# Linear attention and a feed-forward layer in one kernel: d_ff in five stretches with scales of their own, and the first pair's groups taken through them in parts

## The chip, the cores and the metric

The kernel runs on one core of a Trainium2 chip, as one program. The metric is the device time of one execution in microseconds, so smaller is better. Three runs of the kernel before gave 717.43, 718.17 and 720.17; the median is 718.17.

## What is computed

The reference, cut to what matters (8 batches, 8 heads, 576 tokens, heads of 64, 32 memory slots; d_model 512, d_ff 2048):

```python
a = softmax of phi over the 576 tokens             # phi: (8, 8, 576, 32)
k_m = np.einsum('bhsm,bhsd->bhmd', a, k)
v_m = np.einsum('bhsm,bhsd->bhmd', a, v)
attn = softmax of (q @ k_m^T / 8) over the 32 slots
x = attn @ v_m, heads side by side                 # 4608 tokens x 512
h = x @ w_in                                       # 4608 x 2048
g = h * np.cos(h)
out = (g @ w_out).astype(np.float32)               # 4608 x 512
```

Everything comes in as float32 but for the two weight matrices, which the kernel reads as 64-bit floats (pairs of 32-bit words).

## The kernel before, in words

**Work.** The 4608 tokens are taken in 12 groups of 384. Two batches (a pair) make three groups: all of the first group is from the first batch, the second is shared half and half, the third is from the second batch. For each group, d_ff goes by in 16 chunks of 128, so the whole has 192 steps. A step (`gemm1`, `act`, `act_end`, `gemm2`, lines 480 to 543) is:

- TensorE makes hp, 128 d_ff rows by 384 tokens, from the attention weights aT and from vw. vw is v_m folded into w_in beforehand (256 by 2048 for a batch), so that x is never made.
- ScalarE makes u, h in turns plus a quarter (L503). VectorE casts u to whole numbers (L508) and subtracts these (L509). ScalarE takes the sine, which is cos(h) (L513). VectorE multiplies by h (L517). ScalarE casts the product to float16 (L519), and VectorE makes the remainder, a second float16 part (L520).
- Four steps later (`LAG`), TensorE multiplies both parts with w_out into three accumulators of 128 tokens by 512 (L538). After chunk 15, ScalarE copies the three out of PSUM (L554) and they are stored.

**Parts.** From the second group on, a float32 product is made of three float16 products (first by first, first by second, second by first part): 6 matmuls of 384 columns for hp, 9 of 512 for the accumulators. The powers of two that bring the parts into range come from the largest sums of squares of all of w_in and all of w_out (`weight_scale`, L162), so they are known only when all weights are there. The first group doesn't wait for that: it works in float32, 2 matmuls for hp (L485) and 3 for the accumulators (L533), each of which the profile lists as two. Its fold (`fold_first`, L448) gives float32 too.

**Weights.** There are 8 loads of w_in (256 columns each) and 8 of w_out (256 rows each), 1 MB each. `to_float32` (L124) makes float32 of one load with three ScalarE operations (L135, L139, L142, the last with the sum of squares) and two of VectorE (L133, L140). In the first group every step converts one load (`convert_next`, L627). In the second group each step splits a block of w_out (L178, L179) and a quarter of a slice of w_in (L189, L190), whose parts then go by DMA to both halves of the partitions (L200, L201).

**Order.** The kernel is written engine by engine in program order, step by step, with the next batches' attention (`memory`, `attend`) and folds spread over the steps by a table (`jobs`, `folds`). A scheduling layer then fixes the order of each engine's queue; each engine works its own queue in that order, so an instruction that waits holds up all behind it. hp has three PSUM banks, the accumulators three, the small tiles (scores, folds) two. `make_identity` builds the unit matrix ident on GpSimd; the first use of ident is the product `top` (L223), which spreads the maximum of phi.

Of the kernel before, what the change touches and what calls it, by code (L numbers as in the profile page):

```python
# [37 lines left out]
BLK_FIRST = [(0, 256), (256, GT - 256), (GT, S - GT)]  # L38
TWO_PI_BELOW = 6.283185
# [6 lines left out]
def attention_then_ffn(ctx: ExitStack, tc: tile.TileContext, phi, phiT, kv, qT, w_in, w_out, out):  # L46
# [13 lines left out]
    make_identity(nc, ident)  # L60
    # in X, heads of even number hold [k | v] and those of odd number [v | k]
# [5 lines left out]
    w_in_sb = const.tile([P, NP, DF], F32, name="w_in_sb")  # L67
    # w_out: block f + 1 holds rows f * 128 on as float32, later block f their two float16 parts
    wo = const.tile([P, NF + 1, DM], F32, name="wo")

    def wo_parts(f):
        return wo[:, f].bitcast(F16).rearrange("p (w e) -> p w e", w=2)

    vl = const.tile([P, NP, 2, M], F16, name="vl")
# [32 lines left out]
    def load_w_in(j):  # L107
        if j in (2, 3):
            # the space of w_out's last blocks, which come later
            t = wo[:, 13:17] if j == 2 else wo[:, 9:13]  # L110
            t = t.bitcast(I32).rearrange("p c (f t) -> p c f t", t=2)
        else:
            t = ld.tile([P, NP, WS, 2], I32, tag=next_raw(), name=f"raw_in_{j}")
        nc.sync.dma_start(out=t, in_=w_in[:, 2 * WS * j:2 * WS * (j + 1)].rearrange("(c p) (f t) -> p c f t", p=P, t=2))
        loads["in", j] = t

    def load_w_out(j):
        t = ld.tile([P, 2, DM, 2], I32, tag=next_raw(), name=f"raw_out_{j}")
# [3 lines left out]
    sq = const.tile([P, 2, NW], F32, name="sq")  # L122
# [21 lines left out]
    def convert_w_in(j):  # L144
        to_float32(w_in_sb[:, :, j * WS:(j + 1) * WS], loads.pop(("in", j)), sq[:, 0, j:j + 1], j == 1)

    def convert_w_out(j):
        to_float32(wo[:, 2 * j + 1:2 * j + 3], loads.pop(("out", j)), sq[:, 1, j:j + 1])

    # e, a power of two, with every magnitude below 2 e; and 2^14 / e  # L150
# [11 lines left out]
    def weight_scale(kind, name):  # L162
        # halving the exponent of the largest sum of squares
        m = const.tile([P, 1], F32, name=f"m_{name}")
        nc.vector.tensor_reduce(out=m, in_=sq[:, kind], op=ALU.max, axis=AX.X)
        nc.gpsimd.partition_all_reduce(m, m, channels=P, reduce_op=RED.max)
        nc.vector.tensor_scalar(out=m, in0=m, scalar1=2.0, scalar2=2.0 ** -100, op0=ALU.mult, op1=ALU.max)
        nc.vector.tensor_scalar(out=m.bitcast(I32), in0=m.bitcast(I32), scalar1=1, scalar2=None,
                                op0=ALU.logical_shift_right)
        nc.vector.tensor_scalar(out=m, in0=m, scalar1=2.0 ** 63, scalar2=None, op0=ALU.mult)  # L170
        e = const.tile([P, 1], F32, name=f"e_{name}")
        power_of_two(e, m)
        st["e", name] = e
        st["s", name] = to_range(f"s_{name}", const, f"s_{name}", e)

    def w_out_split(f):
        parts, s = wo_parts(f), st["s", "out"]
# [7 lines left out]
    def w_in_split(q, c):  # L185
        if c == 0:
            st["parts"] = ld.tile([P, 2, NP, FS], F16, tag=f"raw{1 + q % 2}", name=f"w_in_parts_{q}")
        parts, s, src = st["parts"], st["s", "in"], w_in_sb[:, c, q * FS:(q + 1) * FS]
        nc.scalar.activation(parts[:, 0, c], src, AF.Copy, scale=s)  # L189
        nc.vector.scalar_tensor_tensor(out=parts[:, 1, c], in0=src, scalar=s, in1=parts[:, 0, c],  # L190
                                       op0=ALU.mult, op1=ALU.subtract)
        if c < NP - 1:
            return
        if q == 0:
            w2 = ld.tile([P, NP, 2, FS], F16, tag="raw0", name="w_in_2_0")
        else:
            w2 = w_in_sb[:, :, (q - 1) * FS:q * FS].bitcast(F16).rearrange("p c (o f) -> p c o f", o=2)
# [6 lines left out]
    # the maximum over the tokens, on all partitions, far ahead of its use  # L204
# [10 lines left out]
    def memory(b):  # L215
        a = loads.pop(("phi", b))
        if b < NT:
            # by the tensor engine, from phi transposed
# [12 lines left out]
        for c0, c1, n in ((0, 2, P), (2, 4, P), (4, 5, S - 512)) if b == 0 else ((0, 4, P), (4, 5, S - 512)):  # L231
# [61 lines left out]
    # the powers of two that bring the two-part float16 operands into range  # L293
    def v_scale(b):
        ev = wk.tile([P, 1], F32, tag="ev", name=f"ev_{b}", bufs=2)
# [3 lines left out]
    def scales(b):  # L299
        E = wk.tile([P, 1], F32, tag="E", name=f"E_{b}", bufs=3)  # L300
        nc.vector.tensor_scalar(out=E, in0=st["ev", b], scalar1=st["e", "in"], scalar2=None, op0=ALU.mult)
        cu = wk.tile([P, 1], F32, tag="cu", name=f"cu_{b}", bufs=3)
        nc.vector.tensor_scalar(out=cu, in0=E, scalar1=2.0 ** -27 / (2.0 * math.pi), scalar2=None, op0=ALU.mult)
        st["E", b], st["cu", b] = E, cu
        if b < 2:
            T = wk.tile([P, 1], F32, tag="T", name=f"T_{b}")
            nc.vector.reciprocal(out=T, in_=E)
            nc.vector.tensor_scalar(out=T, in0=T, scalar1=2.0 ** 13, scalar2=None, op0=ALU.mult)
            st["T", b] = T
        else:  # L310
            # the first part of v_m for both parts of w_in, the second part for the first one alone
# [11 lines left out]
    # attention over the memory: scores with (head, memory) on the partitions; 32 by 32 blocks are  # L323
    # transposed for the softmax over a head's memory, and back
    def attend(b):
        qt, km = loads.pop(("q", b)), st["km", b]
        flat = wk.tile([P, 4 * S], F16, tag="aT", name=f"aT_{b}", bufs=3)
        # the first group works in float32, on the first GT tokens of the first batch
        t32 = GT if b == 0 else 0
        if b == 0:  # L330
            st["aTf"] = flat[:, 0:4 * GT].bitcast(F32).rearrange("p (g x) -> p g x", g=2)
        aT = flat[:, 4 * t32:].rearrange("p (w g x) -> p w g x", w=2, g=2)
# [36 lines left out]
        def back(i):  # L369
            t0, n = BL[i]  # L370
            if t0 < t32:
                for g in range(2):
                    nc.vector.transpose(st["aTf"][:, g, t0:t0 + n], at[:, 2 * t0 + g * n:2 * t0 + (g + 1) * n])
                return
            bk = wk.tile([P, 2, n], F32, tag="back", name=f"back_{b}_{t0}", bufs=4)
            nc.vector.transpose(bk.rearrange("p g x -> p (g x)"), at[:, 2 * t0:2 * (t0 + n)])
            c = slice(t0 - t32, t0 + n - t32)
# [43 lines left out]
    # v_m folded into w_in  # L421
    def fold_psum(b, q, g):
        pv = small_ps(f"pv_{b}_{q}_{g}")
        for i in range(2):
            c = 2 * g + i
            if b < 2:
                nc.tensor.matmul(pv[D * i:D * (i + 1)], lhsT=st["vm", b][:, c],
                                 rhs=w_in_sb[:, c, q * FS:(q + 1) * FS], start=True, stop=True)
        if b >= 2:
            for first in (True, False):  # L430
                for j in range(4):
                    c, o = 2 * g + j // 2, 1 - j % 2
                    nc.tensor.matmul(pv[M * j:M * (j + 1)], lhsT=(st["vp", b] if first else vl)[:, c, o],  # L433
                                     rhs=st["w2", q][:, c, o], start=first, stop=not first, skip_group_check=True)
        return pv

    def split_fold(b, vw, g, src):
        T = st["T", b] if b < 2 else 2.0 ** -15
        nc.scalar.activation(vw[:, 0, g], src, AF.Copy, scale=T)  # L439
        nc.vector.scalar_tensor_tensor(out=vw[:, 1, g], in0=src, scalar=T, in1=vw[:, 0, g],  # L440
                                       op0=ALU.mult, op1=ALU.subtract)

    def fold(b, q, g):
        if g == 0:
            st["vw", b, q] = wk.tile([P, 2, 2, FS], F16, tag="vw", name=f"vw_{b}_{q}", bufs=8)
        split_fold(b, st["vw", b, q], g, fold_psum(b, q, g))

    def fold_first(j):  # L448
        q, r = divmod(j, 2)
        if r == 0:  # L450
            st["vf", q] = wk.tile([P, 2, FS], F32, tag="vw", name=f"vf_{q}", bufs=8)
        pv = small_ps(f"pvf_{j}").rearrange("p (g x) -> p g x", g=2)
        for g in range(2):
            for i in range(2):
# [139 lines left out]
    for _ in mem:  # L594
        pass
# [143 lines left out]
```

## Time and profile before

| | |
|---|---|
| median of three runs | 718.17 us |
| the profiled execution, first to last instruction | 718.0 us |
| mean granted TensorE clock | 0.993 |
| TensorE busy | 694.5 us (97%), 4578 instructions |
| VectorE busy | 569.6 us (79%), 1257 instructions |
| ScalarE busy | 520.3 us (72%), 964 instructions |
| GpSimd busy | 14.6 us (2%), 36 instructions |
| read from and written to memory | 52.31 MB and 9.44 MB |

In the profile PE is TensorE, PEld its loading of weights, DVE VectorE, ACT ScalarE, POOL GpSimd, and SP the queue that issues most DMAs. L503 is line 503 of the kernel. A row of a group has the count behind the x, then the busy time of all, the mean nanoseconds of one, and the idle time of the engine ahead of them with what ended it. A row of a window has for each engine the busy microseconds in that stretch and the number of instructions, then the granted clock, the DMA engines' share and the GB/s. The chain of waits goes back from the last instruction, each time to what released it; "issue" in it is time in which nothing that the profile shows was waited for. Engines in a row of the chain start the next instruction a little before the end of the one before, so a piece there is often shorter than the instruction's own duration.

### The profile page before, as it was taken

What the parts mean: (1) busy time and instruction counts of PE and PEld (TensorE: products, weight loads), DVE (VectorE), ACT (ScalarE), POOL (GpSimd) and SP (SyncE); (2) the same over time, 40 slices, a digit from 0 to 9 for tenths busy, and PEclk for the clock granted to TensorE, in tenths of its full rate; (3) what the DMA queues carried; (4) which work ended last, traced back from release to release, by engine and by line L of the source; (5) the groups of instructions that cost most, each with busy time, mean ns of one, the idle gap of its engine ahead of it and who ended that gap; (6) DMA issues with size and microseconds to landing.
All of it is one profiled execution on the core that took longest, in us unless ns stands there. A gap on an engine that the chain in (4) does not pass through costs nothing.

```text
span 718.0 us, 12024 instructions
## 1 busy us (share of the span) xinstructions
PE 694.5 (97%) x4578; PEld 357.3 (50%) x4578; DVE 569.6 (79%) x1257; ACT 520.3 (72%) x964; POOL 14.6 (2%) x36
## 2 busy tenths in 40 slices
PE   6689999999999999999999999999999999999997
PEld 2345444565454444565444444566444544555553
DVE  2779999998988997589877897669776987676763
ACT  1699999889886875678756685668767785665553
POOL 0000000000000000000000100000000000000000
PEclk9799999999999999999999999999999999999999
DMA  9994981526405300152104310152100000100101
GB/s 282 382 326 159 310 306 30 132 60 188 148 8 160 110 1 1 45 166 67 45 1 135 96 48 1 45 168 67 44 1 1 22 25 1 45 1 1 45 0 45
DMA packets 31417, 66.72 MB, mean 93 GB/s; under 512 B 2176, under 2 KB 10880, under 8 KB 31360
## 3 DMA queue, kind: packets, MB, share of 16 engines
q1 hardware_dynamic: 27040, 58.09, 25.5%
q10 hardware_dynamic: 4320, 7.87, 2.9%
q8 instruction: 36, 0.59, 0.3%
q14 instruction: 21, 0.17, 0.1%
HBM read 52.31 MB, written 9.44 MB: 86 GB/s over the span
## 4 chain that ended last, share of the span: by engine, by line
PE 59%; DVE 20%; ACT 14%; issue 3%; DMA 3%; POOL 0%; SPq 0%; DVEq 0%; ACTq 0%; POOLq 0%
PE acc L538 34%; PE hp L494 18%; PE pv L433 3%; DVE u L517 3%; DVE gp L520 2%; DVE u L509 2%; DMA phi<-in_phi 2%; ACT u L513 2%; DVE gp L508 2%; ACT L513 1%; DVE vw L440 1%; PE psA L248 1%; ACT raw_out L142 1%; DVE wo L179 1%; PE sc L350 1%
## 5 line engine op out<-in xcount | busy, mean ns | idle before, releaser
L538 PE MATMUL acc<-wo,gp 128*128 128x512 f16 x1584 | 371.3, 379 | 0.0
L538 PEld LDWEIGHTS <-gp 128*128 128x128 f16 x1584 | 153.4, 98 | 161.6 <-issue 2.6
L494 PE MATMUL hp<-aT,vw 128*128 128x192 f16 (+1 forms) x1440 | 202.9, 284 | 1.4 <-DVE u L517 1.2
L494 PEld LDWEIGHTS <-vw 128*128 128x128 f16 x1440 | 125.0, 98 | 84.0 <-issue 30.7
L513 ACT ACTIVATE u<-u 128x384 f32<-128x384 f32 x192 | 99.9, 524 | 88.5 <-DVE u L509 87.4
L517 DVE SCALAR_TENSOR_TENSOR u<-hp,u 128x384 f32<-128x384 f32 x176 | 96.9, 553 | 45.8 <-ACT u L513 43.5
L503 ACT ACTIVATE u<-hp,cu 128x192 f32<-128x192 f32 (+1 forms) x240 | 110.9, 492 | 17.0 <-PE hp L494 10.8
L520 DVE TENSOR_TENSOR gp<-u,gp 128x384 f16<-128x384 f32 x176 | 96.6, 552 | 29.8 <-ACT gp L519 29.3
L519 ACT CAST gp<-u 128x384 f16<-128x384 f32 x176 | 89.2, 509 | 40.0 <-DVE u L517 37.9
L509 DVE TENSOR_TENSOR u<-u,gp 128x384 f32<-128x384 f32 x192 | 105.8, 552 | 3.1
L508 DVE CAST gp<-u 128x384 int32<-128x384 f32 x192 | 67.4, 354 | 20.4 <-ACT u L503 18.7
L533 PE MATMUL acc<-wo,gp 128*128 128x512 f32 x96 | 45.5, 599 | 0.2 <-DVE gp L515 0.2
L440 DVE SCALAR_TENSOR_TENSOR vw<-pv,vw 128x512 f16<-128x512 f32 x48 | 33.1, 689 | 4.7 <-ACT vw L439 3.4
L439 ACT ACTIVATE vw<-pv 128x512 f16<-128x512 f32 x48 | 28.3, 591 | 6.4 <-PE pv L433 5.5
L485 PE MATMUL hp<-aT,vf 128*128 128x384 f32 x64 | 26.4, 545 | 4.2 <-DVE gp L515 2.0
L513 ACT ACT_TABLE_LOAD x23 | 29.5, 1283 | 0.4
L533 PEld LDWEIGHTS acc<-wo,gp 128*128 128x128 f32 x96 | 17.2, 190 | 17.4 <-issue 12.9
L248 PE MATMUL psA<-kv,phi 128*32 128x129 f32 (+1 forms) x640 | 23.5, 277 | 0.8 <-ACT phi L238 0.8
L554 ACT ACTIVATE ob<-acc,os 128x512 f32<-128x512 f32 x28 | 18.5, 683 | 8.0 <-PE acc L538 6.1
L248 PEld LDWEIGHTS psA<-kv,phi 128*32 128x32 f32 (+1 forms) x640 | 16.0, 109 | 11.2 <-issue 5.9
L485 PEld LDWEIGHTS hp<-aT,vf 128*128 128x128 f32 x64 | 12.4, 206 | 17.2 <-issue 5.3
L350 PE MATMUL sc<-q,km 128*64 128x256 f32 (+3 forms) x192 | 20.2, 336 | 0.0
(129 smaller groups left out, 553.3 us busy)
## 6 DMA issues: line engine op xcount, KB each, us to landing
kv<-in_kv SPq DMA_DIRECT2D x32, 516.0 KB, 5.8
q<-in_qT SPq DMA_DIRECT2D x8, 1152.0 KB, 5.7
raw_out<-in_w_out SPq DMA_DIRECT2D x8, 1024.0 KB, 5.5
out<-ob ACTq DMA_DIRECT2D x30, 256.0 KB, 2.1
raw_in<-in_w_in SPq DMA_DIRECT2D x6, 1024.0 KB, 7.3
phi<-in_phi SPq DMA_DIRECT2D x8, 512.0 KB, 6.7
w_in_sb<-w_in_parts SPq DMA_DIRECT2D x12, 256.0 KB, 4.6
phiT<-in_phiT SPq DMA_DIRECT2D x4, 576.0 KB, 8.0
```

The source lines that it names most:

```text
L248: nc.tensor.matmul(psA[32 * j:32 * (j + 1), g * KV:(g + 1) * KV], lhsT=a[:n, c, h * M:(h + 1) * M], rhs=kvs[c][:n, h * KV:(h + 1) * KV], s ...
L440: nc.vector.scalar_tensor_tensor(out=vw[:, 1, g], in0=src, scalar=T, in1=vw[:, 0, g], op0=ALU.mult, op1=ALU.subtract)
L494: nc.tensor.matmul(hp[:, c0:c0 + n], lhsT=vw[:, wi, g, fo * P:(fo + 1) * P], rhs=aT[:, ai, g, c1:c1 + n], start=(k == 0), stop=(k == 5))
L503: ins = nc.scalar.activation(u[:, c0:c0 + n], hp[:, c0:c0 + n], AF.Copy, scale=st["cu", b] if grp else 1.0 / (2.0 * math.pi), bias=0.25)
L508: nc.vector.tensor_copy(out=ni, in_=u)
L509: nc.vector.tensor_tensor(out=u, in0=u, in1=ni, op=ALU.subtract)
L513: nc.scalar.activation(u, u, AF.Sin, scale=TWO_PI_BELOW)
L517: nc.vector.scalar_tensor_tensor(out=u, in0=hp[:, :GT], scalar=2.0 ** -17, in1=u, op0=ALU.mult, op1=ALU.mult)
L519: nc.scalar.copy(gp[:, 0], u)
L520: nc.vector.tensor_tensor(out=gp[:, 1], in0=u, in1=gp[:, 0], op=ALU.subtract)
L533: nc.tensor.matmul(accs[grp][t], lhsT=gp[:, t * P:(t + 1) * P], rhs=wo[:, f + 1], start=(f == 0), stop=(f == NF - 1))
L538: nc.tensor.matmul(accs[grp][t], lhsT=gp[:, gi, t * P:(t + 1) * P], rhs=parts[:, wi], start=(f == 0 and gi == 0 and wi == 0), stop=(f == N ...
```

## The change

1. **Stretches with own scales.** d_ff is cut into five stretches of 2, 2, 4, 4 and 4 chunks. Each has its own powers of two, for w_in and w_out at once, made as soon as its loads are converted (`weight_scale(s)`: a maximum on DVE, the all-reduce on GpSimd, five small DVE operations; then `one_scale` and `scales`). w_out's blocks are split right behind that.
2. **All in float16 parts.** The first group is no longer in float32; `fold_first` and `split_first` go, and `fold_32` folds batches 0 and 1 stretch by stretch, straight into float16 parts.
3. **The first pair in parts.** The groups go by in this order: group 0 over stretch 0, over 1, over 2; groups 1 and 2 over stretches 0 to 2; then groups 0, 1 and 2 over stretches 3 and 4. Each of these eight cells ends with its three accumulators being copied out of PSUM. All but the last cell of a group leave a partial sum in SBUF; GpSimd adds them (15 additions of 128 by 512).
4. **A shorter activation.** ScalarE writes the whole number of turns itself (as int32), and VectorE makes h in turns less that number in one operation from PSUM, one for each batch in the group; the quarter turn goes into the sine's bias. The cast on VectorE goes.
5. **The rest.** ident is loaded by DMA, as the first of all loads. The loads of w_in and w_out alternate. The splits of w_in for the later batches stand in steps 22 to 43 (before: 16 to 31). A sequence table (`at_step`) replaces `convert_next`.

The order of the queues is changed most in the first 48 steps. On ScalarE, the rows ahead of the first activation of hp stand so before (`raw` tiles are loads, `sq` the sums of squares, vf and pvf the float32 fold):

```order
L139 ACTIVATE raw_in_0_109<-raw_in_0_109 128x1024
L389 ACTIVATE at_0_237<-at_0_237 128x768
L135 ACTIVATE w_in_sb_87<-raw_in_1_111 128x4x256
L142 ACTIVATE raw_in_0_109,sq_91<-w_in_sb_87 128x1024
L458 COPY vf_0_252<-pvf_0_253 128x2x256
L135 ACTIVATE wo_88<-raw_out_0_113 128x1024
L139 ACTIVATE raw_in_1_111<-raw_in_1_111 128x1024
L139 ACTIVATE raw_out_0_113<-raw_out_0_113 128x1024
L503 ACTIVATE u_0_0_314<-hp_0_0_311 128x384
```

And now, the last rows ahead of it (L146, L150, L153 are the conversion, L216 the first part of a block of w_out, L461 the first part of a fold, T the scale of the stretch):

```order
L146 ACTIVATE wo_85<-wo_85 128x1024
L150 ACTIVATE raw_in_1_115<-raw_in_1_115 128x1024
L150 ACTIVATE wo_85<-wo_85 128x1024
L422 ACTIVATE at_0_246<-at_0_246 128x384
L216 ACTIVATE wo_85<-wo_85,s_w_92 128x512
L146 ACTIVATE w_in_sb_84<-wo_85 128x4x256
L461 ACTIVATE vw_0_0_276<-pv32_0_0_0_277,T_0_271 128x2x256
L216 ACTIVATE wo_85<-wo_85,s_w_92 128x512
L153 ACTIVATE raw_in_1_115,sq_90<-w_in_sb_84 128x1024
L153 ACTIVATE wo_85,sq_90<-wo_85 128x1024
L523 ACTIVATE gp_0_0_388<-hp_0_0_380,cu_0_270 128x384
```

Four loads are wholly converted and a fifth begun ahead of the first activation, where there was one whole load and parts of two; two blocks of w_out are split there too.

On TensorE, at the end of group 0's third cell, the accumulators of this cell (acc_0_4) come behind the folds of batch 1 (pv32_1), now:

```order
L511 MATMUL hp_1_1_819<-aT_0_245,vw_0_0_276 128x192
L485 MATMUL pv32_1_0_0_757<-w_in_sb_84,vm_1_593 64x256 x4
L485 MATMUL pv32_1_1_0_812<-w_in_sb_84,vm_1_593 64x256 x4
L554 LDWEIGHTS gp_0_4_540
L554 MATMUL acc_0_4_0_800<-wo_85,gp_0_4_540 128x512
L554 LDWEIGHTS gp_0_4_540
L554 MATMUL acc_0_4_0_800<-wo_85,gp_0_4_540 128x512
L511 LDWEIGHTS vw_1_0_756
L511 MATMUL hp_1_0_777<-aT_1_641,vw_1_0_756 128x192
```

The bank of acc_0_4_0 comes free by the copy of acc_0_2_0, which on ScalarE stands behind the two copies that those folds wait to make, now:

```order
L153 ACTIVATE raw_in_4_352,sq_90<-w_in_sb_84 128x1024
L461 ACTIVATE vw_1_0_756<-pv32_1_0_0_757,T_1_751 128x2x256
L461 ACTIVATE vw_1_0_756<-pv32_1_1_0_812,T_1_751 128x2x256
L578 ACTIVATE ob_0_0_1_724<-acc_0_2_0_680,os_0_1_2_410 128x512
L578 ACTIVATE ob_0_1_1_727<-acc_0_2_1_681,os_0_1_2_410 128x512
```

Such a turn of the accumulators came once in a group before; there are five more of them now in the first pair.

On GpSimd, the all-reduces stood among memsets before; a row `ISA` without a tile stands where the kind of GpSimd's operations changes; at the one ahead of ident's operation the trace has 9.6 us of `issue`:

```order
L271 MEMSET km_2_1632 128x256
L166 ISA m_in_696<-m_in_696 128x1
L272 MEMSET vm_2_1633 128x256
L166 ISA m_out_782<-m_out_782 128x1
L272 MEMSET vm_3_2184 128x256
```

Now the additions and two such changes stand between them:

```order
L581 ISA
L581 TENSOR_TENSOR sum_0_618<-ob_0_0_1_724,sum_0_618 128x512
L581 TENSOR_TENSOR sum_0_618<-ob_0_1_1_727,sum_0_618 128x512
L581 TENSOR_TENSOR sum_1_621<-ob_0_2_1_730,sum_1_621 128x512
L581 TENSOR_TENSOR sum_0_618<-ob_0_0_2_934,sum_0_618 128x512
L581 TENSOR_TENSOR sum_0_618<-ob_0_1_2_937,sum_0_618 128x512
L581 TENSOR_TENSOR sum_1_621<-ob_0_2_2_940,sum_1_621 128x512
L187 ISA
L187 ISA m_w_3_1066<-m_w_3_1066 128x2
L187 ISA m_w_4_1322<-m_w_4_1322 128x2
```

The all-reduce of the fourth stretch (m_w_3) now comes behind six additions and a change of the loaded kind.

The diff, cut to its core:

```diff
+SEGS = [(0, 2), (2, 2), (4, 4), (8, 4), (12, 4)]
...
-    make_identity(nc, ident)
+    nc.sync.dma_start(out=ident, in_=eye)
...
+    def weight_scale(s):
+
+        j0, j1 = SEGS[s][0] // 2, sum(SEGS[s]) // 2
+        m = wk.tile([P, 2], F32, tag="m_w", name=f"m_w_{s}")
+        if j1 - j0 > 1:
+            nc.vector.tensor_tensor(out=m, in0=sq[:, j0], in1=sq[:, j0 + 1], op=ALU.max)
+        else:
+            nc.vector.tensor_copy(out=m, in_=sq[:, j0])
         nc.gpsimd.partition_all_reduce(m, m, channels=P, reduce_op=RED.max)
...
+        nc.vector.reciprocal(out=s_w[:, s], in_=e)
+        nc.vector.tensor_scalar(out=s_w[:, s], in0=s_w[:, s], scalar1=2.0 ** 14, scalar2=None, op0=ALU.mult)
...
+    def fold_32(b, s):
+        f0, n = SEGS[s]
+        q, r = divmod(f0 * P, FS)
+        vw, T = new_vw(b, q), st["T", b][:, s:s + 1]
+        for part in range(n // 2):
+            pv = small_ps(f"pv32_{b}_{s}_{part}").rearrange("p (g x) -> p g x", g=2)
+            fs = slice(r + part * WS, r + (part + 1) * WS)
+            for g in range(2):
+                for i in range(2):
+                    c = 2 * g + i
+                    nc.tensor.matmul(pv[D * i:D * (i + 1), g], lhsT=st["vm", b][:, c], rhs=w_in_sb[:, q, c, fs],
+                                     start=True, stop=True)
+            split_fold(vw[:, 0, :, fs], vw[:, 1, :, fs], pv, T)
...
-        if grp == 0:
-            for g in range(2):
-                nc.tensor.matmul(hp[:, :GT], lhsT=st["vf", q][:, g, fo * P:(fo + 1) * P], rhs=st["aTf"][:, g],
-                                 start=(g == 0), stop=(g == 1))
-            return hp
...
+            ins = nc.scalar.activation(ni[:, c0:c0 + n], hp[:, c0:c0 + n], AF.Copy, scale=turns, bias=0.25)
...
-        nc.vector.tensor_copy(out=ni, in_=u)
-        nc.vector.tensor_tensor(out=u, in0=u, in1=ni, op=ALU.subtract)
+        for b, t0, c0, n in regions(grp):
+            turns = st["cu", b][:, s:s + 1]
+            nc.vector.scalar_tensor_tensor(out=u[:, c0:c0 + n], in0=hp[:, c0:c0 + n], scalar=turns,
+                                           in1=ni[:, c0:c0 + n], op0=ALU.mult, op1=ALU.subtract)
...
+    def evacuate(grp, t, span=ALL):
         pair, r = divmod(grp, 3)
+        k = 3 * r + t
+        osc = st["os_mid", pair, span] if k == 4 else st["os", 2 * pair + k // 5, span]
+        if span[0] == 0 and span != ALL:
+            nc.scalar.activation(sum_tile(grp, t), accs[grp][t], AF.Copy, scale=osc)
+            return
...
+        if span[0]:
+            to = sum_tile(grp, t) if span[1] < NS else ob
+            nc.gpsimd.tensor_tensor(out=to, in0=ob, in1=sum_tile(grp, t), op=ALU.add)
...
+    A, B_, C, LOW, HIGH = (0, 1), (1, 2), (2, 3), (0, 3), (3, 5)
+    cells = [(0, A), (0, B_), (0, C), (1, LOW), (2, LOW), (0, HIGH), (1, HIGH), (2, HIGH)]
...
+    at_step(0, (convert, 1), (load_next, 3), (ready, 1), (fold_32, 0, 1), (sum_scale, A), (out_scales, 0, A))
+    at_step(2, (sum_scale, B_), (out_scales, 0, B_), (convert_w_in, 2), (load_next,), (convert_w_out, 2), (load_next,))
+    at_step(3, (convert_w_in, 3), (load_next,), (convert_w_out, 3), (load_next,), (ready, 2), (fold_32, 0, 2))
+    at_step(5, (sum_scale, C), (out_scales, 0, C))
+    at_step(8, (scales, 1, 0, 3), (fold_32, 1, 0), (sum_scale, LOW), (out_scales, 0, LOW), (out_scales, 1, LOW))
...
+    for x, j in enumerate((4, 5, 6, 7)):
+        at_step(10 + 3 * x, (convert_w_in, j), (load_next,))
+        at_step(11 + 3 * x, (convert_w_out, j), (load_next,))
+    at_step(15, (ready, 3))
...
+    at_step(22, (ready, 4))
```

More of the change, by code (lines that the diff above doesn't have):

```diff
@@ L448, in fold_first @@
[L448 to L454, printed above, removed]
-                c = 2 * g + i
-                nc.tensor.matmul(pv[D * i:D * (i + 1), g], lhsT=st["vm", 0][:, c],
-                                 rhs=w_in_sb[:, c, j * WS:(j + 1) * WS], start=True, stop=True)
-        (nc.scalar.copy if j < 2 else nc.any.tensor_copy)(out=st["vf", q][:, :, r * WS:(r + 1) * WS], in_=pv)
@@ L651, in attention_then_ffn @@
     gens = {}
     pending, begun = [], []
[L653 to L665 removed]
+    for i, (grp, f, span) in enumerate(steps):
+        for call in before.get(i, ()):
+            call()
```

343 lines of the change are left out of this document (172 added, 171 removed).

## The prediction

> **What bounds the kernel now.** I read the windows first, cut where the pace changes, because a share of the whole span mixes stages.
>
> ```profile
> core 0: us, PE busy (x) PEld busy (x) DVE busy (x) ACT busy (x) POOL busy (x), PEclk, DMA share, GB/s
> 35.00:55.00 20.00, 17.11 (x125) 8.90 (x123) 16.01 (x29) 18.76 (x29) 0.31 (x1) 0.92 0.94 317
> 55.00:98.00 43.00, 42.47 (x175) 20.27 (x166) 40.85 (x82) 42.84 (x62) 1.28 (x4) 1.00 0.71 241
> ...
> 111.00:218.00 107.00, 105.93 (x721) 56.35 (x719) 98.61 (x218) 96.11 (x181) 1.28 (x4) 1.00 0.37 104
> 218.00:702.00 484.00, 482.01 (x3328) 250.41 (x3327) 380.00 (x852) 331.88 (x651) 9.55 (x16) 1.00 0.15 48
> ```
>
> From 218 us on, TensorE alone is full: 482.01 of 484 us, DVE 79%, ACT 69%. From 55 to 98 us three engines are full at once; ACT is idle for 0.16 of 43 us, TensorE for 0.53. So in the front, taking work from TensorE alone buys nothing: ACT would set the same time. The chain of waits says the same. Its pieces there are ACT's weight conversions, end to end; at the close of the kernel they are matmuls, end to end:
>
> ```profile
> 75.67 1.28 ACT L406
> ...
> 79.92 0.38 ACT u L503
> ...
> 91.90 1.06 ACT raw_in L139
> 92.96 1.24 ACT wo L135
> ...
> 94.63 1.17 ACT raw_in L142 x2
> 95.80 0.41 ACT u L513
> ```
> ```profile
> 103.88 0.61 ACT w_in_parts L189
> ...
> 107.61 0.92 ACT vw L439 x2
> ```
> ```profile
> 226.43 1.08 PE hp L494 x6
> ```
> ```profile
> 701.28 0.97 PE hp L494 x6
> 702.25 11.67 PE acc L538 x54
> ```
>
> These pieces run from one start to the next, so they are what an operation costs a full engine. A step in float16 parts costs TensorE 0.97 us for hp and 9 of those 54, 11.67 x 9/54 = 1.94 us, for the accumulators.
>
> Hence two questions: when does ACT let TensorE start its unbroken run, and how much work has TensorE left then?
>
> **The change, part by part. TensorE's work.** The first group's steps:
>
> ```profile
> 102.15 1.45 PE L485 MATMUL hp<-aT,vf 128*128 128x384 f32 x4
> ...
> 105.59 2.74 PE L533 MATMUL acc<-wo,gp 128*128 128x512 f32 x6
> ```
> ```profile
> 671.94 1.14 PE L494 MATMUL hp<-aT,vw 128*128 128x384 f16 x6
> 672.92 2.11 PE L538 MATMUL acc<-wo,gp 128*128 128x512 f16 x9
> ```
>
> A float32 step takes 1.45 + 2.74 = 4.19 us, one in parts 1.14 + 2.11 = 3.25: 0.94 less, 15.0 us over 16 steps. That is the gain if TensorE sets the pace.
>
> **The start.** Today the chain begins on GpSimd:
>
> ```profile
> 1.25 9.56 issue
> 10.80 0.29 POOL ident masks.py:199
> ...
> 11.14 1.22 PE top L223 x4
> ...
> 18.77 0.57 PE psA L248 x16
> ```
>
> The nearest release of `top` other than ident is nmx on DVE, ready at 6.00, so the DMA for ident moves `top` up by at most 5.1 us. What is late next is kv, whose five loads are issued up to 5.07 us; loads of kv land at a median of 6.1 and a maximum of 13.2 us after their issue:
>
> ```profile
> 2.33 2.74 SPq L92 DMA_DIRECT2D kv<-in_kv  x5
> ...
> 4.65 1.35 DVE L220 TENSOR_REDUCE nmx<-phiT 128x2 f32<-128x1152 f32 x1 [2.96 <-DMA phiT<-in_phiT]
> ...
> 21.50 0.27 ACT L275 ACTIVATE km<-tpx 64x128 f32<-64x128 f32 x1 [6.85 <-PE tpx L268]
> ```
> ```profile
> DMA to landing us min/median/max: 3.5/6.1/13.2
> ```
>
> The last one may land as late as 18.3, when the last fifth of psA (18.77) gains 0.5 us. Between 0.5 and 5.1 I take 3: ACT's first work of that chain, km, moves from 21.5 to about 18.4.
>
> **ACT up to the second turn of the accumulators.** TensorE's unbroken run can begin when ACT has copied acc_0_2_0 out (L578; front, third place). In ACT's queue there stand ahead of this, from 18.4 us on: 11 each of L146 and L150 (before L135, L139) and 9 of L153 (L142), the conversions, at 1.24, 1.06 and 1.17: 13.6 + 11.7 + 10.5; 14 first parts of splits and folds at about 0.6 (0.61, and 0.92 for two on top of a neighbour): 8.4; 7 copies at 0.38, 7 sines at 0.41, 7 casts of the same size at 0.40: 8.3; 3 copies of accumulators at 0.57 (683 ns in their row, less the 0.11 by which the sine's 524 ns stand above 0.41): 1.7; 4 table loads at 1.28: 5.1; 13 smaller ones of both attentions at about 0.5: 6.5. The sum is 65.8, so without any wait this point is reached at 18.4 + 65.8 = 84.2 us.
>
> ```profile
> L513 ACT ACTIVATE u<-u 128x384 f32<-128x384 f32 x192 | 99.9, 524 | 88.5 <-DVE u L509 87.4
> ...
> L554 ACT ACTIVATE ob<-acc,os 128x512 f32<-128x512 f32 x28 | 18.5, 683 | 8.0 <-PE acc L538 6.1
> ```
>
> But ACT must wait there for something that it hardly waits for now: the scales. Each goes from ACT's sum of squares to DVE, to GpSimd, through DVE again and back to ACT's splits. Before, one such chain lay beside the conversions:
>
> ```profile
> L165 DVE TENSOR_REDUCE m_in<-sq x1: 161/161/161, 95.8 to 95.8; 128x1 f32<-128x8 f32 x1
> ...
> L152 DVE TENSOR_SCALAR e_in<-m_in x1: 144/144/144, 99.4 to 99.4; 128x1 f32<-128x1 f32 x1
> ```
>
> It took 3.6 us for five small operations, because large ones stand between them in DVE's queue. Three such chains lie ahead of the turn, with about ten small DVE operations each, and what waits behind them in ACT's queue are the splits, then conversions; of TensorE, the fold and hp. I price each at 3 us of ACT standing still, 9 in all; 0 if conversions always fill it, 14 if each costs what the longer chain takes. The turn comes at 84.2 + 9 = 93 us (84 to 98).
>
> **What TensorE has left there.** I compare with the kernel before at 98 us, where it had begun the fourteenth step (what is left in float32, the old folds of batch 0 and of batch 1):
>
> ```profile
> 98.00:126.00 28.00, 17.20 (x36) 1.00 0.44 145
> ```
> ```profile
> 98.00:126.00 28.00, 4.30 (x13) 1.00 0.44 145
> ```
> ```profile
> 0.00:98.00 98.00, 9.90 (x64) 0.95 0.85 288
> ```
> ```profile
> 98.00:228.00 130.00, 8.62 (x28) 1.00 0.43 125
> ```
>
> These are L533, L485, L456 and L427. Up to the fourth group, the old queue holds after that point 28 accumulator steps in parts and, in float32, 17.20 + 4.30 us; the new one, from the turn on, 40 accumulator steps, 48 more hp matmuls of 384 and 12 fewer of 192 columns (worth 7 steps of hp), and 40 fold matmuls (80 records at 9.90/64 us) against 8.62. Difference: 12 x 1.94 + 7 x 0.97 + 12.4 - 17.2 - 4.3 - 8.6 = +12.4 us. All else in the first pair and all behind it is the same work.
>
> **Sum.** End = 718.0 + 12.4 + (93 - 98) + further waits. For these I add 2.5: five more turns of the accumulators at some 0.5, as 3 copies at 0.57 hide mostly behind the hp matmuls (0.97) between two cells; bounds -2 and +10. Below nothing, because of the shorter activation: the cast (L508 below)
>
> ```profile
> L517 DVE SCALAR_TENSOR_TENSOR u<-hp,u 128x384 f32<-128x384 f32 x176 | 96.9, 553 | 45.8 <-ACT u L513 43.5
> ...
> L508 DVE CAST gp<-u 128x384 int32<-128x384 f32 x192 | 67.4, 354 | 20.4 <-ACT u L503 18.7
> ```
>
> frees DVE for 67 us, and the operation that takes L509's place costs the like of L517. But behind 218 us TensorE idles for 2 of 484 us, so this is worth 2 us at most. The result is 728 us. The profiled span, 718.0, is the median of the runs (718.17) to 0.02%, so it holds for both. A measurement of this kernel can tell about 0.5% (3.6 us) from no change.
>
> GpSimd's additions have no like in this trace; its nearest rows are
>
> ```profile
> L211 POOL PARTITION_ALL_REDUCE mx<-mx x4 | 4.5, 1117 | 14.4 <-DVE mx L210 14.4
> ...
> L271 POOL MEMSET km<- 128x256 f32 x8 | 2.5, 312 | 64.6 <-PE sc L350 64.6
> ```
>
> so 0.3 (the memset) to 2.2 us each (twice the all-reduce), I take 1.1 by the all-reduce, and 9.56 us at each change of kind. Nobody waits for a sum, but DVE waits for the all-reduce of the fourth stretch, which stands behind six additions and a change. DVE's queue behind that wait holds the activations. I think it is covered mostly (the run has four steps of products in stock), and leave it within the +10. The Trainium skill (GPSIMD Engine Reference, Instruction dispatch) gives approximately 6 us for the first call to freshly loaded code; the chain's row here shows 9.56. By the 6, the rival on this change, below, would end 3.6 us earlier.
>
> **Rivals.** *TensorE sets the pace* (faster): the 15.0 us count if the turn comes by 80 us; then 718 + 12.4 - 18 - 2 = 710. For it speaks that ACT's waits before 35 us could be used; against it, that ACT's queue alone needs until 84, at the price it has when it is full. Chance 0.10. *ACT never waits* (no change): the turn at 84 to 87, 718 + 12.4 - 12.5 - 0 = 718. For it: ACT idled 0.16 us in 43 before. Against: the scales, three times. Chance 0.15. *DVE waits for GpSimd* (much slower): the change of kind and the six additions ahead of m_w_3 are waited for in full, 9.6 + 6 x 1.1 = 16 us, which goes through DVE to TensorE: 728 + 16 = 744. It decides when the additions end later than the sums of squares of the fourth stretch. Against it, the additions come in two bursts of three and the first burst can be long done. Chance 0.06. *Additions shut DVE out* (much slower): while GpSimd adds, operations of DVE with two inputs in SBUF stand still, 15 x 1.1 = 17 us: 745. For it, nothing: GpSimd's 16 instructions between 218 and 702 us were memsets and all-reduces, and no row shows DVE held by them; against it, most of DVE's work reads PSUM, and DVE is not full everywhere. Chance 0.04. The Trainium skill (SBUF — State Buffer, SBUF: two separate sides) states such a rule: GpSimd and VectorE share a pair of ports under an exclusive lock, and VectorE's operations with two SBUF inputs are shut out while GpSimd reads; no run here shows it yet.
>
> **How the numbers follow.** Forecast 728 with 0.65; its own ends are the turn at 88 to 98 and waits of 0 to 8: 720 to 738. The range takes in *ACT never waits* and reaches to the lower part of the two on GpSimd: 715 to 742; outside lie the faster case and the upper parts of the last two, under 0.2. Faster by over 0.5%: 0.10. Within: 0.15 and a little of the forecast's low end, 0.17. Slower: 0.73.
>
> **What would show it.** Right: ACT 80 to 90% busy from 40 us to the copy of acc_0_2_0, this copy at 88 to 98, TensorE under 60% busy before it and over 97% from there on; the fourth group's first hp some 5 to 15 us later than before, where it begins at 226.43; unchanged pace behind it. Wrong: the copy by 82 us or TensorE full before it (then faster); or TensorE with holes between 100 and 230 us that end on DVE (then GpSimd or DVE, and later than 738).

## The result and the profile after

The changed kernel takes 743.41 us (median of 4 runs, 741.8 to 745.41), the kernel before 718.75 beside it: the ratio is 1.0331, 95% interval 1.0301 to 1.0362. It is slower, as forecast, but by 25 us instead of 10, and outside the range of 715 to 742. The profiled execution spans 743.0 us.

The windows of the changed kernel, cut at the moments that the prediction named (columns as before):

```profile
core 0: us, PE busy (x) PEld busy (x) DVE busy (x) ACT busy (x) POOL busy (x), PEclk, DMA share, GB/s
35.00:55.00 20.00, 14.53 (x50) 5.44 (x51) 19.33 (x43) 19.93 (x29) 0.37 (x1) 0.65 0.75 255
55.00:91.70 36.70, 22.02 (x201) 12.65 (x200) 31.25 (x80) 34.16 (x52) 1.27 (x3) 0.88 0.76 260
91.70:98.00 6.30, 5.29 (x17) 2.29 (x17) 6.25 (x8) 5.64 (x8) 4.16 (x3) 0.50 0.34 138
98.00:140.00 42.00, 39.77 (x249) 22.25 (x248) 37.69 (x76) 40.82 (x79) 4.60 (x4) 0.98 0.31 101
140.00:170.00 30.00, 29.36 (x163) 14.63 (x162) 28.18 (x68) 30.00 (x55) 0.67 (x2) 1.00 0.21 49
170.00:218.00 48.00, 45.52 (x362) 27.04 (x361) 43.03 (x96) 37.13 (x69) 4.88 (x7) 0.96 0.66 162
218.00:260.00 42.00, 41.56 (x311) 20.60 (x310) 33.72 (x77) 29.75 (x56) 5.77 (x6) 1.00 0.39 115
260.00:275.00 15.00, 9.86 (x57) 4.20 (x55) 9.36 (x18) 7.03 (x13) 3.71 (x3) 0.86 0.17 63
275.00:290.00 15.00, 14.96 (x82) 6.83 (x81) 11.59 (x23) 11.37 (x24) 0.31 (x1) 0.92 0.01 2
290.00:702.00 412.00, 408.55 (x2877) 215.80 (x2876) 300.02 (x635) 289.61 (x557) 6.81 (x12) 1.00 0.14 46
```

Three things are new. TensorE works 36.6 of 56.7 us between 35 and 91.7 (before, it was full from 55 on). ACT is busy for about 90% or more of every window up to 170 us (before, it was full up to 111 us, and then busy for 26.72 of 29 and 27.64 of 30 us). And a hole stands at 260 to 275 us, TensorE 9.86 of 15, where the prediction had an unchanged pace; behind this hole and behind 91.7 us the granted clock is low.

The second copy of accumulators out of PSUM, which the prediction had at 93 us, in the timeline of ACT, and TensorE at the same place:

```profile
90.95 1.27 ACT L578 ACTIVATE ob<-acc,os 128x512 f32<-128x512 f32 x2
```
```profile
83.58 1.95 PE L485 MATMUL pv<-w_in_sb,vm 128*64 128x256 f32 x16
91.69 1.01 PE L554 MATMUL acc<-wo,gp 128*128 128x512 f16 x2 [6.17 <-ACT ob L578]
```

It came at 90.95, and TensorE, which had waited 6.17 us for it, went on at 91.69. So the forecast's first half held to about 2 us. What failed lies behind it.

The hole at 260 us, in the timeline of all engines (a row: start, duration, engine and line; in brackets the idle time ahead and what ended it):

```profile
255.71 0.31 POOL L312 MEMSET km<- 128x256 f32 x1 [5.42 <-PE sc L387]
...
257.67 1.83 ACT L578 ACTIVATE ob<-acc,os 128x512 f32<-128x512 f32 x3
...
265.07 3.71 POOL L581 TENSOR_TENSOR ob<-ob,sum 128x512 f32<-128x512 f32 x3 [9.04 <-issue]
...
266.35 2.79 ACTq L584 DMA_DIRECT2D out<-ob  x3
...
269.19 1.52 ACT L523 ACTIVATE gp<-hp,cu 128x384 int32<-128x384 f32 x3 [5.95 <-POOL ob L581]
269.81 1.67 DVE L528 SCALAR_TENSOR_TENSOR u<-hp,cu,gp 128x384 f32<-128x384 f32 x3 [1.02 <-ACT gp L523]
...
273.35 4.00 PE L511 MATMUL hp<-aT,vw 128*128 128x384 f16 x12 [5.14 <-DVE u L536]
...
277.14 2.30 PE L554 MATMUL acc<-wo,gp 128*128 128x512 f16 x9
...
279.28 1.14 PE L511 MATMUL hp<-aT,vw 128*128 128x384 f16 x6
```

Read it from the top. GpSimd ends a memset at 256.0 and changes its kind of operation, 9.04 us without a visible instruction. ACT has copied the accumulators out by 259.5, but the additions run only from 265.07. Their sums are stored from ACT's own queue (L584), so ACT's queue stands before the first store until 266.35, and all three activations of hp behind the stores wait until 269.19. VectorE waits for these, and TensorE for VectorE, 5.14 us. Then twelve matmuls of hp take 3.79 us (273.35 to 277.14), where six take 0.97 (279.28 to the next at 280.25) at full clock: half speed, which loses another 1.9 us. The same stands at 201.77 us, with 4.86 us of ACT and 2.3 of TensorE.

**The sum again.** TensorE's time is counted from 91.7 us instead of 98: -6.3. The work counted in the prediction: +12.4. Idle time of TensorE from there to 702 us, by the windows, 15.4 us against 1.1 + 2.0 before: +12.3. Half clock, read from the starts of the matmuls as above: about 3.6 us lost up to 100, 1.6 at 209.3 to 212.5, 2.0 at 273.4 to 277.4, so about 7. In all +25.4; the spans differ by 25.0. This is an account of TensorE's time, not of causes: where another engine sets the pace, slow matmuls can fill time that would otherwise be a wait.

### The profile page after: what moved, and what is told of

Same layout as the page of the kernel before. It is cut to its first block, busy times and chain, and to the rows that moved or that the text cites. A ratio compares the mean times of both kernels' runs of the same rounds, so it can differ in the third digit from the quotient of the medians.

```text
span 743.0 us, 12147 instructions
## 1 busy us (share of the span) xinstructions
PE 686.9 (92%) x4690; PEld 359.0 (48%) x4690; DVE 559.7 (75%) x1200; ACT 539.1 (73%) x985; POOL 35.0 (5%) x52
## 4 chain that ended last, share of the span: by engine, by line
PE 60%; DVE 15%; ACT 15%; DMA 6%; POOL 2%; issue 2%; ACTq 0%; SPq 0%; POOLq 0%; DVEq 0%
PE acc L554 35%; PE hp L511 18%; DMA phi<-in_phi 3%; PE pv L470 3%; ACT u L533 2%; ACT gp L523 2%; DVE u L528 2%; DMA raw_in<-in_w_in 2%; PE psA L289 2%; DVE u L536 2%; DVE gp L539 2%; ACT gp L538 1%; POOL ob L581 1%; DVE rs L398 1%; ACT raw_out L153 1%
## 5 line engine op out<-in xcount | busy, mean ns | idle before, releaser
L554 PE MATMUL acc<-wo,gp 128*128 128x512 f16 x1728 | 409.2, 382 | 12.8 <-ACT ob L578 6.2
L554 PEld LDWEIGHTS <-gp 128*128 128x128 f16 x1728 | 168.2, 98 | 191.5 <-issue 14.0
L511 PE MATMUL hp<-aT,vw 128*128 128x384 f16 (+1 forms) x1536 | 229.4, 294 | 18.0 <-DVE u L536 9.1
L533 ACT ACTIVATE u<-u,quarter 128x384 f32<-128x384 f32 x192 | 115.9, 614 | 69.6 <-DVE u L528 69.0
L536 DVE SCALAR_TENSOR_TENSOR u<-hp,z,u 128x384 f32<-128x384 f32 x184 | 111.4, 613 | 59.3 <-ACT u L533 58.8
L528 DVE SCALAR_TENSOR_TENSOR u<-hp,cu,gp 128x192 f32<-128x192 f32 (+1 forms) x256 | 124.4, 510 | 34.0 <-ACT gp L523 32.7
L523 ACT ACTIVATE gp<-hp,cu 128x192 int32<-128x192 f32 (+1 forms) x256 | 119.0, 496 | 32.0 <-PE hp L511 14.7
L461 ACT ACTIVATE vw<-pv 128x512 f16<-128x512 f32 x48 | 28.4, 591 | 4.4 <-PE pv L470 3.8
L485 PE MATMUL pv<-w_in_sb,vm 128*64 128x256 f32 x128 | 19.6, 431 | 12.7 <-DVE T L350 7.6
L289 PEld LDWEIGHTS psA<-kv,phi 128*32 128x32 f32 (+1 forms) x640 | 16.3, 109 | 12.6 <-issue 6.8
L470 PE MATMUL pv<-w_in_sb,vp 128*32 128x512 f16 x192 | 19.2, 389 | 1.3 <-DVE at L389 1.2
L470 PE MATMUL pv<-w_in_sb,vl 128*32 128x512 f16 x192 | 19.1, 379 | 0.0
## 6 DMA issues: line engine op xcount, KB each, us to landing
out<-ob ACTq DMA_DIRECT2D x30, 256.0 KB, 2.1
w_in_sb<-w_in_parts SPq DMA_DIRECT2D x16, 256.0 KB, 5.0
```

The lines of the kernel that those rows point to most:

```text
L289: nc.tensor.matmul(psA[32 * j:32 * (j + 1), g * KV:(g + 1) * KV], lhsT=a[:n, c, h * M:(h + 1) * M], rhs=kvs[c][:n, h * KV:(h + 1) * KV], s ...
L485: nc.tensor.matmul(pv[D * i:D * (i + 1), g], lhsT=st["vm", b][:, c], rhs=w_in_sb[:, q, c, fs], start=True, stop=True)
L511: nc.tensor.matmul(hp[:, c0:c0 + n], lhsT=vw[:, wi, g, fo * P:(fo + 1) * P], rhs=aT[:, ai, g, t0:t0 + n], start=(k == 0), stop=(k == 5))
L523: ins = nc.scalar.activation(ni[:, c0:c0 + n], hp[:, c0:c0 + n], AF.Copy, scale=turns, bias=0.25)
L528: nc.vector.scalar_tensor_tensor(out=u[:, c0:c0 + n], in0=hp[:, c0:c0 + n], scalar=turns, in1=ni[:, c0:c0 + n], op0=ALU.mult, op1=ALU.subt ...
L533: nc.scalar.activation(u, u, AF.Sin, scale=TWO_PI_BELOW, bias=quarter)
```

## The experiments

### Stores and additions

Theory *Stores*: the new hole is made by stores that wait in ACT's queue for GpSimd. Rival *Front*: what counts is the work left when TensorE's run begins, and the hole only displaces other waits. Rival *Port*: GpSimd's additions hold VectorE up.

```diff
-            (nc.sync if grp >= 10 else nc.scalar).dma_start(
+            (nc.sync if grp >= 10 or span[0] else nc.scalar).dma_start(
```

> The changed kernel, but the nine stores behind a GpSimd addition are issued by SP instead of ACT. Theory Stores: a store in ACT's queue waits for the addition, and all activations stand behind it; this cost TensorE 2.3 us of waiting at 207 to 210 us and 5.1 at 273 us, and a clock of 0.5 for 3.3 and 4.1 us behind them (half of it lost, 3.7 us). Both go, so some 11 us less: 743 to about 732. Rival Front: the lost time is the work that is left when TensorE's unbroken run begins, and these waits only displace others; 743 to 740. Rival Port: the additions themselves hold VectorE up wherever they stand; 743, with the waits of VectorE as long as before.

Measured: 735.39 us, 8.0 less by the medians and 9.6 by the spans (733.4; the profiled run of the changed kernel, at 744.74, was 1.3 above its median); 1.0218 of before (1.0190 to 1.0245). Its window at the place of the hole, and GpSimd's timeline there:

```profile
260.00:275.00 15.00, 15.00 (x88) 6.83 (x85) 13.90 (x27) 10.38 (x23) 4.62 (x3) 1.00 0.14 54
```
```profile
262.29 4.62 POOL L581 TENSOR_TENSOR ob<-ob,sum 128x512 f32<-128x512 f32 x3 [9.01 <-ACT gp L523]
```

The additions are still as late, with 9.01 us of idle ahead of them, but TensorE is full at full clock. *Stores* is right, somewhat smaller than its 11 us.

```diff
+        elif span[0]:
+            to = sum_tile(grp, t) if span[1] < NS else ob
+            nc.vector.scalar_tensor_tensor(out=to, in0=accs[grp][t], scalar=osc, in1=sum_tile(grp, t),
+                                           op0=ALU.mult, op1=ALU.add)
...
-        if span[0]:
-            to = sum_tile(grp, t) if span[1] < NS else ob
-            nc.gpsimd.tensor_tensor(out=to, in0=ob, in1=sum_tile(grp, t), op=ALU.add)
```

> The changed kernel, but the 15 additions are made by VectorE straight from PSUM (accumulator times its scale plus the partial sum, one operation), in place of ACT's copy and GpSimd's addition; so GpSimd doesn't change its kind of operation in between. Stores: as with the stores on SP, about 732, since the same waits go; ACT has 15 copies of 0.68 us less, VectorE 15 operations of about 0.75 us more, both with room after 218 us. Front: 740 to 743. Port: some 2 us less than the kernel with its stores on SP, as GpSimd reads nothing while VectorE works.

Measured: 735.13 us, 1.0207 (1.0181 to 1.0232). The stores are on ACT's queue here, but their sums are ready; so it takes both, the late addition and the queue. No more is won than with the stores on SP. That doesn't settle *Port*: the run also gives VectorE 15 operations of 0.73 to 0.74 us, 11 us in all, which can hide a gain of 2 us. TensorE went on earlier at the second turn of the accumulators, and that brought nothing:

```profile
87.79 4.48 PE L554 MATMUL acc<-wo,gp 128*128 128x512 f16 x20 [1.60 <-DVE sum L580]
```
```profile
91.00:98.00 7.00, 3.96 (x21) 2.26 (x20) 7.00 (x17) 5.60 (x10) 0.00 (x0) 0.86 0.00 0
```

In that window VectorE is busy for all of the 7 us, right behind three of its additions (87.00 to 90.45). ACT waits for it, and TensorE behind both:

```profile
92.15 0.63 ACT L411 ACTIVATE aT<-back 128x512 f16<-128x512 f32 x1 [3.47 <-DVE back L409]
```
```profile
96.82 0.96 PE L511 MATMUL hp<-aT,vw 128*128 128x192 f16 x5 [3.04 <-DVE u L536]
```

So here VectorE took back what the earlier turn had won. The earlier turn alone didn't help.

### The start

```diff
-    nc.sync.dma_start(out=ident, in_=eye)
+    make_identity(nc, ident)
```

> The changed kernel, with ident built on GpSimd again, as before the change. Theory Front (the moment at which ACT copies the second set of accumulators out sets when TensorE's unbroken run begins): km 3.8 us later (17.7 to about 21.5 us), that copy 3 to 4 us later than 91, and the end as much later: 746 to 747. Rival: between 20 and 90 us ACT's waits for the scales and folds absorb it; 743 to 744, with the copy at 91 to 92.

Measured: 748.43 us, 1.0384 (1.0355 to 1.0414), a span of 747.8, 4.8 longer (3.8 by the two ratios to the kernel before). ACT begins km at 21.50 (17.66 with the DMA) and copies the accumulators 3.0 us later:

```profile
21.50 0.27 ACT L317 ACTIVATE km<-tpx 64x128 f32<-64x128 f32 x1 [7.11 <-PE tpx L310]
```
```profile
93.92 1.27 ACT L579 ACTIVATE ob<-acc,os 128x512 f32<-128x512 f32 x2
```

*Front* holds for this edit: what begins later in the front ends later, and its waits didn't absorb it. (ACT's first conversion began only 0.7 us later, at 22.08 instead of 21.39; then ACT waited 2.82 us for VectorE. The hole that stood at 273 us was 0.9 us longer too, 6.04.)

The same edit the other way round, in the kernel before:

```diff
-    make_identity(nc, ident)
+    nc.sync.dma_start(out=ident, in_=eye)
```

> The kernel before, with the one edit that ident is loaded by DMA. If the early start counts there as well: ACT is full from 35 us on, all of it begins some 3 us earlier, and the end is 714 to 716. Rival: the loads keep their pace (DMA over 94% busy up to 55 us) and ACT waits for them instead; 718, within 0.3%.

Measured: 718.06 against 720.21 us of before on that chip, 0.9975 (0.9962 to 0.9989). km came only 2.0 us earlier there (19.49), and the gain of 2.15 us is about that. It lies at the edge of both forecasts, 2 to 4 us less and within 0.3%, so it doesn't decide between them; by the interval it isn't nothing.

### What fills ACT in the front

The price of 9 us that the prediction put on three scales was tested by leaving the scales' chains out (constants set at the start in their place):

```diff
+    for kind, e in ((0, 1.0), (1, 0.5)):
+        nc.vector.memset(e_w[:, :, kind], e)
+        nc.vector.memset(s_w[:, :, kind], 2.0 ** 14 / e)
...
     def weight_scale(s):
+        return
```

> The changed kernel with its stores on SP (735.4, the second copy of accumulators at 90.2 us), and the weights' scales as constants set at the start, so the five chains of maximum, all-reduce and small VectorE operations are left out; the squares are still summed. It tests a term of the prediction, 9 us of ACT waiting for three scales. If the term is right: that copy at about 81, the end at 726. Rival: conversions and ACT's own queue hide the chains; the copy at 88 to 90, the end at 733 to 735.

Measured: 736.9 us, 1.0230 (1.0186 to 1.0274), a span of 734.2, no gain. Leaving out ACT's sums of squares as well:

```diff
-        nc.scalar.activation(low.bitcast(F32), dst, AF.Square, accum_out=sq_to)
```

> The same with constant scales, and ACT's sum of squares left out of each conversion as well (16 operations of 1.13 us, nine of them ahead of the second copy of accumulators, the others up to about 170 us). Front, with ACT's queue as what sets it: that copy 10 us earlier than with constant scales alone, the end as much earlier, and 5 to 8 more if ACT also sets the pace between 98 and 170 us; 12 us or more between the two. Rival: the loads or TensorE take over at once; the end 0 to 3 us earlier.

Measured: 726.98 us, 1.0080 (1.0054 to 1.0106), a span of 723.4. The copies of accumulators, first start in each, of the one with constant scales and then of the one without squares:

```profile
L567 ACT ACTIVATE ob<-acc,os x37: 666/687/708, 91.8 to 730.4; 128x512 f32<-128x512 f32 x37
```
```profile
L566 ACT ACTIVATE ob<-acc,os x37: 666/687/698, 83.0 to 719.6; 128x512 f32<-128x512 f32 x37
```

Without the chains the copy is no earlier (91.8, with them 90.2); without the squares it is 8.8 us earlier, and the span 10.8 shorter, a little under the 12 expected. So it is ACT's work, not its waits for scales.

Is that so in the kernel before as well? The same cut there, with constants for the sums and the rest of the chain kept:

```diff
+    nc.vector.memset(sq[:, 0], 2.4)
+    nc.vector.memset(sq[:, 1], 0.6)
...
-        nc.scalar.activation(low.bitcast(F32), dst, AF.Square, accum_out=sq_to)
```

> The kernel before, with ACT's 16 sums of squares (1.15 us each) left out and two constants in their place, the rest of the scales' chain kept. In the changed kernel the same cut, beside constant scales, took 10.8 us off the profiled span. If ACT's queue sets the pace up to 170 us in the changed kernel alone, TensorE (42.5 of 43 us busy at 55 to 98, 28.7 of 29 at 111 to 140) sets it here, and the gain is 0 to 4 us. If ACT is the bound of the front in both kernels, 8 to 11 us less.

Measured: 717.06 against 720.34 us, 0.9957 (0.9940 to 0.9975): 3 us. Before, ACT and TensorE are full side by side, and 18 us less on ACT buy 3; after the change they buy 10.8. The change has made ACT the bound of the front, where TensorE had been as full before.

### The activation

The old activation in the changed kernel with its stores on SP:

```diff
-            ins = nc.scalar.activation(ni[:, c0:c0 + n], hp[:, c0:c0 + n], AF.Copy, scale=turns, bias=0.25)
+            ins = nc.scalar.activation(u[:, c0:c0 + n], hp[:, c0:c0 + n], AF.Copy, scale=turns, bias=0.25)
...
+        nc.vector.tensor_copy(out=ni, in_=u)
+        nc.vector.tensor_tensor(out=u, in0=u, in1=ni, op=ALU.subtract)
...
-        nc.scalar.activation(u, u, AF.Sin, scale=TWO_PI_BELOW, bias=quarter)
+        nc.scalar.activation(u, u, AF.Sin, scale=TWO_PI_BELOW)
```

> The changed kernel with its stores on SP, and the activation of before: ACT writes turns as float32, VectorE casts and subtracts, the sine has no quarter as its bias. ACT's sine takes 0.52 us in place of 0.61; VectorE has 0.35 + 0.55 a step in place of 0.61. If ACT alone sets the pace up to 170 us: 80 steps of 0.09, so 7 us less, 728. If VectorE (28.2 of 30 us busy at 140 to 170) is as near: 80 steps of 0.29 more on it, at least half of it on the path, 742 to 755. I expect the second.

Measured: 746.2 us, 1.0362 (1.0321 to 1.0404), some 10 us slower than with the shorter one (span 742.9 against 733.4).

```profile
98.00:140.00 42.00, 37.15 (x236) 21.66 (x235) 41.18 (x80) 39.23 (x75) 6.21 (x5) 0.96 0.28 95
```

VectorE is full now (41.18 of 42 us), ACT less. Behind ACT, VectorE is the next bound of the front, and the shorter activation is worth 10 us there.

The shorter activation in the kernel before:

```diff
-            ins = nc.scalar.activation(u[:, c0:c0 + n], hp[:, c0:c0 + n], AF.Copy,
+            ins = nc.scalar.activation(ni[:, c0:c0 + n], hp[:, c0:c0 + n], AF.Copy, scale=turns, bias=0.25)
...
-        nc.vector.tensor_copy(out=ni, in_=u)
-        nc.vector.tensor_tensor(out=u, in0=u, in1=ni, op=ALU.subtract)
+            nc.vector.scalar_tensor_tensor(out=u[:, c0:c0 + n], in0=hp[:, c0:c0 + n], scalar=turns,
+                                           in1=ni[:, c0:c0 + n], op0=ALU.mult, op1=ALU.subtract)
```

> The kernel before with the shorter activation alone (ACT writes the whole turns as int32, VectorE makes the rest in one operation for each batch, the quarter turn is the sine's bias). The prediction's term: worth 0 to 2 us, so 716 to 718.5. Rival: the sine with a bias from a tile takes 0.09 us longer, and ACT is full up to 170 us: 48 steps and more, 3 to 4 us slower.

Measured: 718.62 against 720.83 us, 0.9967 (0.9948 to 0.9985): 2.2 us, by the interval 1.1 to 3.7. That is the upper end of the prediction's term (0 to 2 us); the longer sine doesn't show in the time. Both edits in the kernel before together:

> The kernel before with ident by DMA and with the shorter activation, the two parts of the change that each took 0.25 to 0.33% off it. If their gains add up: 0.993 to 0.995 of before. If both use the same slack: 0.996 to 0.998.

Measured: 718.49 against 720.34 us, 0.9974 (0.9956 to 0.9992). The two don't add up (their product would be 0.994, below the interval), which fits two edits that use the same slack but doesn't show it. This and each part alone are faster than the kernel before by some 2 us, and by their intervals none stands above the others.

## Why the prediction was wrong

**TensorE's work in float16 parts and the 12.4 us that are left.** Right as far as the sum can tell: -6.3 + 12.4 and the waits and clock read from the rows close to 0.4 us. No run tested the 12.4 alone, but the windows bear it out: TensorE is busy for 632.0 us from 91.7 us to the end, and for 612.9 from 98 us before. Of these 19.1 us, 7 are half clock, and 12 are left.

**The start.** 3 us were forecast for km; it came 3.8 us earlier (17.66). Undone, it cost 4.8 by the spans.

**The turn at 93 us.** It came at 90.95 with the right sum of work: ACT was busy for 66.30 of the 72.50 us from 18.4 on, where the sum had 65.8. The reason given for the rest was wrong. ACT's waits, from the km of 17.66 to the turn:

```profile
ACT w_in_sb L146 <- DMA raw_in<-in_w_in: 3.2, 1, 3.2
ACT raw_out L153 <- DVE wo L151: 1.1, 2, 0.8
ACT gp L538 <- DVE u L536: 1.0, 1, 1.0
ACT wo L150 <- DVE s_w L193: 0.4, 1, 0.4
```
```profile
18.40:90.90 72.50, 41.49 (x282) 21.01 (x281) 64.61 (x154) 66.30 (x93) 2.69 (x6) 0.80 0.82 290
```

Half is the first load, and only 0.4 us is a scale: chains of small operations were hidden by conversions, as constant scales showed. The 9 us were too much by 3 and in the wrong place, so that the turn came so near is in part luck. The signs named beside it were missed: from 40 us to the copy ACT was busy for 95% (forecast 80 to 90) and TensorE for 64% (under 60). The fourth group's first hp begins at 242.76, 16.3 us later than before and just outside the 5 to 15, as a part of the waits and the low clock lies ahead of it.

**"Further waits", the step that failed.** The sum had 2.5 us (-2 to +10); it was 19, 12.3 of waiting and about 7 of clock. The sentence that failed is "Nobody waits for a sum". ACT did, because the last sum of a group is stored by a DMA from ACT's queue, and a store there waits for its data with all activations behind it. The change puts GpSimd between the copy and the store; the prediction followed the additions to the next all-reduce on GpSimd, but not the store that reads them. *Stores* is worth 8 us by the medians and 9.6 by the spans. With the stores on SP the kernel takes 735.4 us, inside the range but still 7 above 728. That rest lies in the front: there TensorE idles for 7.5 us between 98 and 218 us (before, 1.1).

The second omission is the clock. Three waits of TensorE have slow matmuls behind them, as at 273 us: 5.14 us of waiting and 1.9 us lost at half clock. This was read from the trace of the changed kernel, not tried in a run of its own. The Trainium skill (TensorE: Matmul & The Clock Gate, Part 1: The HAM clock gate) has the clock fall to half after an idle window of about 3.4 us and come back after as long a busy one. Half clock for 4.1 us behind a wait of 5.14 agrees. Behind 91.7 us it held for some 8 us, and at 209.3 it came behind two waits of 1.23 and 1.02 us with 0.6 us of work between, less idle time than that window.

**"From the turn on, TensorE sets the pace."** Wrong up to 170 us: ACT is busy for 30.00 of 30 us at 140 to 170. TensorE's holes there (2.9 us between 98 and 170) fit that. VectorE is close behind: the prediction gave the shorter activation 2 us at most, from the idle time behind 218 us, and in the front of the changed kernel, with its stores on SP, it is worth 10.

**The rivals.** *ACT never waits* gave the turn at 84 to 87 and no loss; it didn't happen. *DVE waits for GpSimd* had the right engine and the wrong waiter: the all-reduces of m_w cost VectorE 1.1 us in all. That its 744 is so near to the 743.4 measured is luck. The sign of being wrong, holes of TensorE that end on DVE and an end later than 738, did come, at 207 to 210 us. *Additions shut DVE out* exists, but smaller than its 17 us. While GpSimd adds (200.48 to 204.2), in the timeline:

```profile
200.48 3.71 POOL L581 TENSOR_TENSOR ob<-ob,sum 128x512 f32<-128x512 f32 x3 [7.29 <-ACT at L439]
201.77 2.83 ACTq L584 DMA_DIRECT2D out<-ob  x3
201.94 1.05 DVE L399 TENSOR_SCALAR rs<-rs 128x16 f32<-128x16 f32 x1
203.32 1.42 DVE L404 TENSOR_TENSOR at<-at,rs 128x512 f32<-128x512 f32 x1
```

Between 300 and 700 us these two forms take 0.69 and 0.15 us, by the groups of VectorE's instructions (count behind the x, then busy time and mean ns):

```profile
L404 DVE TENSOR_TENSOR at<-at,rs 128x512 f32<-128x512 f32 x4 | 2.8, 688 | 0.1
...
L399 DVE TENSOR_SCALAR rs<-rs 128x16 f32<-128x16 f32 x4 | 0.6, 151 | 0.0
```

So these two are held for 0.7 to 0.9 us. Four more are held for 0.8 to 1.1 us each beside the additions at 93 to 112 us, where VectorE has little room. TensorE waited for the first of them, which takes 0.68 us elsewhere:

```profile
93.23 1.60 DVE L412 SCALAR_TENSOR_TENSOR aT<-back,aT 128x512 f16<-128x512 f32 x1
```
```profile
94.89 0.96 PE L511 MATMUL hp<-aT,vw 128*128 128x192 f16 x5 [0.93 <-DVE aT L412]
```

In all it is 5.4 us of VectorE. Three of the six, L404 and L412 among them, have two inputs in SBUF, in agreement with the rule of the Trainium skill that the prediction cited (SBUF — State Buffer, SBUF: two separate sides). The other three, L399 among them, read one tensor, and for these the prediction named no rule. What all this costs the kernel is open: the run with the additions on VectorE removes it, but loads VectorE with 11 us.

## What to carry to other kernels

When a change puts an engine between a producer and a store, ask from which queue the store is issued, and what stands behind it there: a DMA that waits for its data holds up the engine that issues it. An engine that is off the critical path can be late by one change of kind (7 to 9 us here), and that is enough. Where two engines are full side by side, taking work from one and adding to the other moves the bound: test it by cutting the same work in both versions, as the sums of squares did (3 us before, 10.8 after).

## What the runs showed of the hardware

GpSimd's first addition behind memsets and all-reduces came 9.04 and 9.01 us after the operation ahead of it, with nothing visible between. The price is not fixed: at 200.48 us the same gap was 7.29 us, though the first copy to be added was done by 195.1. And not each change has one: the memset behind these additions began at 204.13, at once. An addition of 128 by 512 on GpSimd takes 1.26 us (1254 to 1266 ns for nine of them); two of the other six, beside VectorE's held operations, took 1.72 and 1.76.

A bias from a tile makes ACT's sine longer by 91 ns, after and before:

```profile
L533 ACT ACTIVATE u<-u,quarter x192: 587/614/653, 44.2 to 729.6; 128x384 f32<-128x384 f32 x192
```
```profile
L513 ACT ACTIVATE u<-u x192: 504/523/590, 42.1 to 707.3; 128x384 f32<-128x384 f32 x192
```

That is 17 us of ACT over 192 steps for an edit that is called shorter; it was shorter on VectorE alone.
